# Staging places taken in the order of their last use, and the raw weights behind the change of MoE loaded at other times and from another queue

## The chip, the cores and the metric

The kernel runs on one core of a Trainium2 chip. The metric is the device time of one execution in microseconds (us), the median of several runs. The core has TensorE (PE in the profile), VectorE (DVE), ScalarE (ACT) and GpSimd (POOL), and SyncE (SP), which here only issues DMAs. A DMA can be issued by SP or by ACT. It then stands among that engine's own instructions: one that has to wait holds up all that stands behind it on the same engine.

## The reference

Attention over 4 batches of 576 tokens gives x (2304 x 512). A first mixture of experts (4 experts, width 1024, ReLU, outputs weighted by domain_probs) follows, and then one dense pair of layers of width 2048 with ELU, called the second MoE here.

```python
def _moe_ref(x, domain_probs, w1, w2) -> np.ndarray:
    ...
    for e in range(E):
        h = np.maximum(x @ w1[e], 0.0)
        out += p[:, e:e + 1] * (h @ w2[e])
    return out.astype(np.float32)
...
def _moe2_ref(x, w_in, w_out) -> np.ndarray:
    h = x @ w_in
    alpha = 1.0
    g = np.where(h > 0.0, h, alpha * (np.exp(np.minimum(h, 0.0)) - 1.0))
    return (g @ w_out).astype(np.float32)
```

## The kernel before

**Steps.** Attention and expert 0 come first. The rest is 30 steps, `i` = 0 to 29, in `STEPS`: step `i` is half unit `s` = i // 3 (512 hidden features: half an expert, or a quarter of the second MoE) for block `b` = i % 3 (768 tokens). `S_MOE` is 6, so steps 0 to 17 are experts 1 to 3 and steps 18 to 29 are the second MoE; the change of MoE is between steps 17 and 18. A step has two passes (`fp`) of seven Strassen products `p` = 0 to 6 (L996, 6 matmuls of 384 columns each) for the first layer. After products 1, 3 and 5 of each pass stands a `chunk` of the step before (L1043 to L1045, 12 matmuls of 512 columns: the second layer for 128 tokens).

**Hooks.** A chunk calls `hook2` four times, so a step has 24 hooks. `at2(i, k, fn)` puts `fn` at hook `k` of step `i`; `k` may run on into later steps, so that hook 42 set from step 18 is hook 18 of step 19. All work beside the products is spread over the engines in this way, and each engine runs its part in the order in which it was written.

**Precision.** Every fp32 operand is held as two parts, high and low: a copy to the rounded type (ACT or POOL) and a subtraction (DVE or POOL).

**The turn.** The second MoE needs the output of the first one transposed, in seven Strassen operands per block. `turn_steps(b, c)` makes them for nine groups of 128 + 128 tokens in steps 16 to 19: PE transposes (L837), ACT copies back (L838), POOL forms differences (L860), and `emit` splits an operand into high and low in a staging place (copy L845 or L847, subtraction L851) and stores it to `xs` in DRAM from SP (L852). There are 63 emits, numbered 0 to 62 here by `stage_n`. The subtraction and the store of one emit are written just ahead of the next hook function of the turn.

**Staging places.** `staged(n)` chooses the place of emit n. Up to the start of step 18 there are six places: `y`, `qh`, `ql`, the two halves of the tile `ek`, and a part of `extra`. From step 18 on, where ELU wants `y`, `qh`, `ql` and `extra` itself, there are four (the halves of `ek` and of one tile `r` of the pool `stg`), and from hook 9 of step 18 on six (a second `r`). The choice is `n % 6` or `n % len(stage)`. An emit waits until the last store from its place has landed.

**Ring loads.** `ring_load` (L664) brings a product's operand back from `xs`, high (`xh`) and low (`xl`) part, from SP. The seven of step i + 1 are issued in the second pass of step i: the first two at product 0, then one at each of products 1 to 5, so the one for product 5 at product 4. For the second MoE a ring load has to wait for the stores that it reads.

**Raw weights.** `w_load(s, p, layer)` (L679 to L683) loads a pair of raw weight tiles, 256 KB each, into an `r` of the same pool `stg`, which has two buffers; it is issued by ACT. `w1_steps` splits and combines the first layer's weights, `w2_step` the second layer's (copies on ACT, L735, subtractions on POOL, L736). In most half units the second layer's weights of s + 1 come first (loads at hooks 2 and 10, `w2_step` at 25 and 29) and the first layer's at 34 and 38. For s = 6 (`S_MOE`), both second-layer loads are at hook 42, right behind the last emit of the turn at hook 41, with `w2_step` at 47 and 49, and the first layer's loads at 52 and 54.

**ELU.** L1020 to L1031: three ACT functions of a PSUM bank, DVE combines, ACT and DVE split the result. The bank can be written by PE again when DVE has read it (L1026).

Of the kernel before, what the change touches and what calls it, by code (L numbers as in the profile page):

```python
# [9 lines left out]
F32R = mybir.dt.float32r  # L10
# [9 lines left out]
def tile_attention_moe_moe(  # L20
# [13 lines left out]
    nc = tc.nc  # L34
    NP_, CP, NC, P = q.shape
    D, S = P // 2, NC * CP
    NT, DM = out.shape
# [39 lines left out]
    TB, FS = 384, 4  # L77
    NB = NT // (2 * TB)
    STEPS = [(s, b) for s in range((NU - 1) * FPU // FS) for b in range(NB)]
    S_MOE = (E - 1) * FPU // FS  # L80
# [11 lines left out]
    stg = ctx.enter_context(tc.tile_pool(name="stg", bufs=2))  # L92
    hp_ = ctx.enter_context(tc.tile_pool(name="hp", bufs=1))
    kvp = ctx.enter_context(tc.tile_pool(name="kvp", bufs=1))
    tmp = ctx.enter_context(tc.tile_pool(name="tmp", bufs=1))
# [396 lines left out]
    def bank(which):  # L492
        pool = ps_h if which == "h" else ps[which]
        return pool.tile([P, ps["wide"] if which == "m" else 1, 512], F32, tag=which, name=which)
# [5 lines left out]
    t = bank("o")  # L500
# [62 lines left out]
    for i in range(NP_):  # L563
        late = i >= NPAIR
        t = K_START[i - NPAIR] if late else HALF_STEP * i
# [103 lines left out]
    def w_load(s, p, layer):  # L669

        if (s, p, layer) == (0, 1, 1):
            r = tmp.tile([P, 2, DM], F32, tag="ek", name="r")
        else:
            r = stg.tile([P, 2, DM], F32, tag="r", name="r")
        for j in range(2):
            u, c = divmod(FPU + s * FS + 2 * p + j, FPU)
            if u >= E:
                src = scratch[(u - E) * FPU + c, :, layer, :]
                nc.scalar.dma_start(out=r[:, j, :], in_=src)  # L679
            elif layer == 0:  # L680
                nc.scalar.dma_start(out=r[:, j, :].rearrange("p (d f) -> p d f", d=KD), in_=w1[u][c])
            else:
                nc.scalar.dma_start(out=r[:, j, :], in_=w2[u][c * P : (c + 1) * P, :])  # L683
        (w1r, w2r)[layer][s, p] = r

    def w1_steps(s, p):

        r, t = [], []

        def begin():  # L690
            r.append(w1r.pop((s, p)).rearrange("p j (d f) -> p j d f", d=KD))
            new()

        def new():
            t.extend(wp.tile([P, 2, KD, P], F32R, tag="w1", name="w1s") for _ in range(2))
            if len(t) == 4:
                w1s[s, p] = dict(
                    A11=(t[0], 0), A12=(t[0], 2), A22=(t[1], 0),
                    S2=(t[2], 0), S4=(t[2], 2), S3=(t[3], 0), S1=(t[3], 2),
                )  # L700

        def src(k):
            return (r[0][:, 0], r[0][:, 1, 2:], r[0][:, 0], r[0][:, 1])[k]

        def dst(k, hl):
            return t[k][:, hl, :2] if k == 1 else t[k][:, hl]

        def hi(k):
            nc.scalar.activation(out=dst(k, 0), in_=src(k), func=AF.Copy)

        tt = nc.vector.tensor_tensor

        def lo(k):
            tt(out=dst(k, 1), in0=src(k), in1=dst(k, 0).bitcast(F32), op=ALU.subtract)

        def sums1():
            f1, f2 = r[0][:, 0], r[0][:, 1]
            tt(out=f2[:, 2:], in0=f2[:, :2], in1=f2[:, 2:], op=ALU.add)
            tt(out=f2[:, :2], in0=f1[:, :2], in1=f2[:, :2], op=ALU.subtract)

        def sums2():
            f1, f2 = r[0][:, 0], r[0][:, 1]
            tt(out=f1[:, :2], in0=f2[:, 2:], in1=f1[:, :2], op=ALU.subtract)
            tt(out=f1[:, 2:], in0=f1[:, 2:], in1=f1[:, :2], op=ALU.subtract)

        return {
            0: lambda: (begin(), hi(1), hi(0)), 1: lambda: lo(1), 2: lambda: lo(0), 3: sums1, 4: lambda: (new(), hi(3)),
            5: lambda: (lo(3), sums2()), 6: lambda: hi(2), 7: lambda: lo(2),
        }

    def w2_step(s, p):
        r = w2r.pop((s, p))
        for j in range(2):
            t = wp.tile([P, 2, DM], F32R, tag="w2", name="w2s")
            nc.scalar.activation(out=t[:, 0], in_=r[:, j], func=AF.Copy)  # L735
            nc.gpsimd.tensor_tensor(out=t[:, 1], in0=r[:, j], in1=t[:, 0].bitcast(F32), op=ALU.subtract)  # L736
            w2s[s, 2 * p + j] = t


    SH = 24  # L740
# [3 lines left out]
    def at2(i, k, fn):  # L744
        timed2.setdefault(i * SH + k, []).append(fn)
# [6 lines left out]
    for b in range(NB):  # L752
        need = min(NP_, -(-2 * TB * (b + 1) // S) * NPAIR)
        t = 66 + 36 * b
# [22 lines left out]
    for i, (s, b) in enumerate(STEPS):  # L777
        more = s + 1 < len(STEPS) // NB
        if b == 0:
            for n, fn in w1_steps(s, 1).items():  # L780
                if s == 0 and n < 4:
                    at(204 + n, fn)
                else:
                    at2(i, n - 4 * (s == 0), fn)
        if not more:
            continue
        if b == 0:

            at2(i, 2 if s != S_MOE else 42, lambda s=s: w_load(s + 1, 0, 1))
            at2(i, 10 if s != S_MOE else 42, lambda s=s: w_load(s + 1, 1, 1))  # L790
            at2(i, SH + (1 if s != S_MOE else 23), lambda s=s: w2_step(s + 1, 0))
            at2(i, SH + (5 if s != S_MOE else 25), lambda s=s: w2_step(s + 1, 1))
            at2(i, SH + (10 if s != S_MOE else 28), lambda s=s: w_load(s + 1, 0, 0))
            at2(i, SH + (14 if s != S_MOE else 30), lambda s=s: w_load(s + 1, 1, 0))
        if b == 2:
            for n, fn in w1_steps(s + 1, 0).items():
                at2(i, 12 + n, fn)


    stage = []  # L800

    def staged(n):

        now = hook2_n[0] - NB * S_MOE * SH

        def two(pool, tag):
            t = pool.tile([P, 2, 2, 2 * P], F32R, tag=tag, name="stage")
            stage.extend([t[:, 0], t[:, 1]])

        if not stage:  # L810
            two(tmp, "ek")
        if now < 0:
            k = n % 6
            if k < 3:
                return tmp.tile([P, 2, 2 * P], F32R, tag=("y", "qh", "ql")[k], name="staged")
            if k == 5:
                return extra[:, TB : TB + DM].bitcast(F32R).rearrange("p (l n) -> p l n", l=2)
            return stage[k - 3]
        while len(stage) < (4 if now < 9 else 6):
            two(stg, "r")  # L820
        return stage[n % len(stage)]

    stage_n, stores = [0], []

# [4 lines left out]
    def turn_steps(b, c):  # L829
        j1, j2 = 6 * b + c, 6 * b + c + 3  # L830
        a1, a2 = acc(j1), acc(j2)
        q4 = {"B11": a1[:, : 2 * P], "B21": a1[:, 2 * P :], "B12": a2[:, : 2 * P], "B22": a2[:, 2 * P :]}

        def turn(a):
            t = bank("o")[:, 0, :]
            for d in range(KD):
                nc.tensor.transpose(t[:, d * P : (d + 1) * P], a[:, d * P : (d + 1) * P], ident)  # L837
            nc.scalar.activation(out=a, in_=t, func=AF.Copy)  # L838

        def emit(op, at_):  # L840
            t, x = staged(stage_n[0]), q4[at_]
            stage_n[0] += 1
            k, early = stage_n[0] % 7, hook2_n[0] < NB * S_MOE * SH
            if early or k % 2 == 0:
                nc.scalar.activation(out=t[:, 0], in_=x, func=AF.Copy)  # L845
            else:
                nc.gpsimd.tensor_copy(out=t[:, 0], in_=x)  # L847
            eng = nc.vector if early or k not in (1, 5) else nc.gpsimd

            def rest():  # L850
                eng.tensor_tensor(out=t[:, 1], in0=x, in1=t[:, 0].bitcast(F32), op=ALU.subtract)  # L851
                nc.sync.dma_start(  # L852
                    out=xs[1, b, OPS.index(op)].rearrange("p l (d n) -> p l d n", d=2)[..., c * P : (c + 1) * P],
                    in_=t.bitcast(F32).rearrange("p l (d n) -> p l d n", d=2),
                )

            stores.append(rest)

        def diff(o, x, y):
            nc.gpsimd.tensor_tensor(out=q4[o], in0=q4[x], in1=q4[y], op=ALU.subtract)  # L860

        return [
            lambda: turn(a1), lambda: turn(a2), lambda: emit("B11", "B11"), lambda: diff("B11", "B12", "B11"),
            lambda: emit("T1", "B11"), lambda: diff("B11", "B22", "B11"), lambda: emit("T2", "B11"),
            lambda: emit("B21", "B21"), lambda: (diff("B12", "B22", "B12"), diff("B21", "B21", "B11")),
            lambda: emit("T3", "B12"), lambda: emit("B22", "B22"), lambda: emit("T4", "B21"), lambda: None,
        ]

    for b in range(NB):
        i = NB * (S_MOE - 1) + b + 1  # L870
# [75 lines left out]
    for step in START.split():  # L946
        n, i = step[:-1], int(step[-1])
# [27 lines left out]
    extra = kvp.tile([P, NPAIR * 2 * P], F32, tag="kv", name="extra")  # L975
# [186 lines left out]
```

## Time and profile before

| | us |
|---|---|
| median of 3 runs (lowest to highest) | 1261.67 (1260.92 to 1263.71) |
| the profiled execution | 1260.91 |
| its span in the trace | 1259.1 |
| PE busy | 1217.0 |
| DVE / ACT / POOL busy | 804.4 / 505.5 / 190.0 |
| an undisturbed step (727.18 to 758.46) | 31.28 |

Times in the trace count from the span's start. "Busy" of PE includes time at a lower granted clock; the idle time of an engine matters only where PE waits for it. A step begins with the first matmul of its product 0; steps 15 to 21 begin at 727.18, 758.46, 791.51, 825.44, 869.67, 907.67 and 952.49.

### The profile page before, as it was taken

To read this page: it belongs to the slowest core of one execution; us is meant where nothing else is said; L and a number is where in the kernel's file an instruction comes from. 1 tells how busy PE (TensorE), PEld (TensorE's weight loads), DVE (VectorE), ACT (ScalarE), POOL (GpSimd) and SP (SyncE) were. 2 spreads that over 40 slices of the span, in tenths; PEclk is the share of its full clock that TensorE was granted. 3 is DMA by queue.
4 is the path that set the end of the run, shared out by engine and by line. 5 is a ranking of instruction groups with operands and counts; after the bars stand their busy time and mean duration, and the time that the engine had idled before them with its cause. 6 is when DMAs were issued, how large, how long until landed. Compare 5 with 4: busy or idle time off the path is not lost.

```text
span 1259.1 us, 18264 instructions
## 1 busy us (share of the span) xinstructions
PE 1217.0 (97%) x6526; PEld 1083.4 (86%) x6526; DVE 804.4 (64%) x1514; ACT 505.5 (40%) x1105; POOL 190.0 (15%) x194
## 2 busy tenths in 40 slices
PE   7799999999999999999999999989779999999998
PEld 6688889889999988999998999878678898998996
DVE  6866776356676676676676663666546567567564
ACT  6544553232222222222222222545466656556552
POOL 4522552011001001001001001244310100100000
PEclk8899999999999999999999999999989999999999
DMA  7434557628677677677677675879855556555541
GB/s 234 131 110 137 185 194 253 219 79 324 234 264 271 237 254 257 234 274 257 241 260 256 232 264 206 273 231 290 275 180 206 182 199 207 192 194 172 184 178 75
DMA packets 152603, 272.19 MB, mean 216 GB/s; under 512 B 12864, under 2 KB 72768, under 8 KB 152512
## 3 DMA queue, kind: packets, MB, share of 16 engines
q1 hardware_dynamic: 131776, 224.87, 52.0%
q10 hardware_dynamic: 20736, 46.15, 10.4%
q8 instruction: 52, 0.85, 0.3%
q14 instruction: 39, 0.32, 0.1%
HBM read 224.83 MB, written 46.14 MB: 215 GB/s over the span
## 4 chain that ended last, share of the span: by engine, by line
PE 86%; DVE 5%; DMA 3%; ACT 3%; issue 2%; SPq 1%; POOL 0%; ACTq 0%; POOLq 0%; DVEq 0%
PE m L996 16%; PE h L996 16%; PE o L1045 12%; PE o L1044 12%; PE o L1043 12%; PE o L879 7%; PE h L879 7%; DMA xs<-stage 2%; PE m L264 1%; PE m L356 1%; ACT t L1022 1%; PE m L333 1%; DVE g L1026 1%; PE o L837 0%; DMA r<-in_w_dram 0%
## 5 line engine op out<-in xcount | busy, mean ns | idle before, releaser
L996 PE MATMUL m<-xh,w1s 128*128 128x384 f32 x840 | 247.6, 341 | 17.2 <-DVE g L1026 10.5
L996 PE MATMUL h<-xh,w1s 128*128 128x384 f32 x840 | 246.0, 339 | 5.0 <-ACT m L1077 4.3
L996 PEld LDWEIGHTS m<-xh,w1s 128*128 128x128 f32 x840 | 156.3, 190 | 22.6 <-DVE g L1026 10.8
L996 PEld LDWEIGHTS h<-xh,w1s 128*128 128x128 f32 x840 | 155.4, 189 | 11.4 <-ACT m L1077 7.1
L736 POOL TENSOR_TENSOR w2s<-r,w2s 128x512 fp32r<-128x512 f32 x40 | 53.8, 1364 | 691.5 <-ACT w2s L735 480.9
L1043 PE MATMUL o<-w2s,xl 128*128 128x512 f32 x360 | 141.8, 394 | 1.8 <-ACT xl L1030 1.8
L1045 PE MATMUL o<-w2s,xl 128*128 128x512 f32 x360 | 142.9, 397 | 0.0
L996 PE MATMUL m<-xl,w1s 128*128 128x384 f32 x420 | 142.5, 339 | 0.0
L1044 PE MATMUL o<-w2s,xl 128*128 128x512 f32 x360 | 142.4, 395 | 0.0
L996 PE MATMUL h<-xl,w1s 128*128 128x384 f32 x420 | 141.5, 337 | 0.0
L1023 DVE SCALAR_TENSOR_TENSOR extra<-extra,t 128x384 f32<-128x384 f32 x96 | 54.2, 565 | 128.6 <-ACT t L1022 128.6
L879 PE MATMUL o<-w2t,hpa 128*128 128x512 f32 x432 | 118.0, 402 | 1.2 <-DVE hpa L911 1.0
L879 PE MATMUL h<-xh,w1t 128*128 128x256 f32 (+1 forms) x512 | 112.1, 298 | 0.1
L879 PEld LDWEIGHTS h<-xh,w1t 128*128 128x128 f32 x512 | 86.1, 192 | 5.2 <-POOL w1t L402 0.3
L879 PEld LDWEIGHTS o<-w2t,hpa 128*128 128x128 f32 x432 | 76.1, 190 | 15.1 <-DVE hpa L911 2.4
L996 PEld LDWEIGHTS m<-xl,w1s 128*128 128x128 f32 x420 | 79.8, 190 | 3.4
L996 PEld LDWEIGHTS h<-xl,w1s 128*128 128x128 f32 x420 | 79.3, 189 | 3.2
L1045 PEld LDWEIGHTS o<-w2s,xl 128*128 128x128 f32 x360 | 67.9, 189 | 16.2 <-DVE xl L1031 1.8
L1043 PEld LDWEIGHTS o<-w2s,xl 128*128 128x128 f32 x360 | 68.3, 190 | 15.5 <-ACT xl L1030 3.7
L1044 PEld LDWEIGHTS o<-w2s,xl 128*128 128x128 f32 x360 | 68.0, 189 | 12.1
L879 PE MATMUL h<-xl,w1t 128*128 128x256 f32 (+1 forms) x256 | 77.3, 302 | 0.0
L1051 DVE SCALAR_TENSOR_TENSOR accB<-o,pn,accB 128x512 f32<-128x512 f32 x60 | 44.9, 749 | 50.5 <-PE o L1045 50.4
(188 smaller groups left out, 2275.4 us busy)
## 6 DMA issues: line engine op xcount, KB each, us to landing
xh<-xs SPq DMA_DIRECT2D x210, 384.0 KB, 5.1
xl<-xs SPq DMA_DIRECT2D x210, 384.0 KB, 5.8
r<-in_w_dram ACTq DMA_DIRECT2D x48, 256.0 KB, 3.7
xs<-stage SPq DMA_DIRECT2D x47, 256.0 KB, 3.3
x<-in_w_in_dram ACTq DMA_DIRECT2D x16, 512.0 KB, 5.5
x<-in_w_out_dram ACTq DMA_DIRECT2D x16, 512.0 KB, 4.8
r<-scratch ACTq DMA_DIRECT2D x32, 256.0 KB, 3.7
xs<-xh SPq DMA_DIRECT2D x21, 384.0 KB, 3.6
```

Of the source, the lines that this page charges most:

```text
L264: nc.tensor.matmul(o, ek[:n, ks], vs, start=(c == 0), stop=(c == len(k_chunks) - 1))
L333: nc.tensor.transpose(t[:, a - halves[0], c * CP : (c + 1) * CP], qt[:CP, 3 * a + c, :], ident[:CP, :CP])
L356: nc.tensor.matmul(t[:, a, :HALF], kv[:, l, :], r[:, a, :], start=(n == 0), stop=(n == 2))
L736: nc.gpsimd.tensor_tensor(out=t[:, 1], in0=r[:, j], in1=t[:, 0].bitcast(F32), op=ALU.subtract)
L879: nc.tensor.matmul(out, lhsT, rhs, **kw)
L996: nc.tensor.matmul(dst, t[:, wl, c + dl, :], x[xl_][:, dl, :], start=(n == 0 and p < 2), stop=(n == 5), skip_group_check=True,)
L1022: nc.scalar.activation(out=t, in_=m, func=AF.Tanh, scale=-0.5)
L1023: nc.vector.scalar_tensor_tensor(out=e_, in0=e_, scalar=1.0, in1=t, op0=ALU.add, op1=ALU.mult)
L1043: nc.tensor.matmul(o, gh, w[:, 0, :], start=(f == 0), stop=False)
L1044: nc.tensor.matmul(o, gh, w[:, 1, :], start=False, stop=False)
L1045: nc.tensor.matmul(o, gl, w[:, 0, :], start=False, stop=(f == FS - 1))
L1051: nc.vector.scalar_tensor_tensor(out=a, in0=o, scalar=pn[:, j, e : e + 1], in1=a, op0=ALU.mult, op1=ALU.add)
```

## The change

Three things are changed.

1. `staged` no longer counts. It keeps the places in a list, takes the first and puts it at the end, so that the place used longest ago is next. In the first phase the order becomes `y`, `qh`, `ql`, `extra`, `ek`, `ek`. When the tile `r` comes in, its halves go to the front of the list.
2. For the half unit behind the change of MoE (s + 1 = 7), the loads of the first layer's raw weights come first, both at hook 42; the second layer's come later, at hooks 70 and 82, with their `w2_step` at 77 and 91. For s + 1 = 8 the second layer's loads move from hooks 2 and 10 to 21 and 23, the `w2_step` from 25 and 29 to 29 and 33, and the first layer's loads from 34 and 38 to 38 and 42.
3. The loads of the first layer's raw weights for half unit 7 are issued by SP and not by ACT.

```diff
+        q = nc.sync if (s, layer) == (S_MOE + 1, 0) else nc.scalar
         for j in range(2):
...
-                nc.scalar.dma_start(out=r[:, j, :], in_=src)
+                q.dma_start(out=r[:, j, :], in_=src)
...
-            at2(i, 2 if s != S_MOE else 42, lambda s=s: w_load(s + 1, 0, 1))
...
+            a2, b2, c2, d2, a1, b1 = (2, 10, 25, 29, 34, 38)
+            if s == S_MOE:
+                a1, b1, a2, c2, b2, d2 = (42, 42, 70, 77, 82, 91)
+            elif s == S_MOE + 1:
+                a2, b2, c2, d2, a1, b1 = (21, 23, 29, 33, 38, 42)
+            at2(i, a2, lambda s=s: w_load(s + 1, 0, 1))
...
-        if now < 0:
-            k = n % 6
-            if k < 3:
-                return tmp.tile([P, 2, 2 * P], F32R, tag=("y", "qh", "ql")[k], name="staged")
-            if k == 5:
-                return extra[:, TB : TB + DM].bitcast(F32R).rearrange("p (l n) -> p l n", l=2)
-            return stage[k - 3]
-        while len(stage) < (4 if now < 9 else 6):
-            two(stg, "r")
-        return stage[n % len(stage)]
...
+        if "ek" in stage:
+            stage[-1:] = two(tmp, "ek")
+        if now >= 0 and any(isinstance(t, str) for t in stage):
+            stage[:] = two(stg, "r") + [t for t in stage if not isinstance(t, str)]
+        if now >= 9 and len(stage) == 4:
+            stage[:0] = two(stg, "r")
+        t = stage.pop(0)
+        stage.append(t)
```

The first place is on ACT at the start of step 18, where the number of places changes: `stage_7033` is the tile `ek`, `stage_7472` the first `r`; the three stage rows are emits 24, 26 and 27 (emit 25 is copied by POOL). Before:

```order
L709 ACTIVATE w1s_7461<-r_6982 128x512
L845 ACTIVATE stage_7033<-accA_92 128x256
L838 ACTIVATE accB_93<-o_7477 128x512
L845 ACTIVATE stage_7472<-accA_92 128x256
L838 ACTIVATE accB_93<-o_7493 128x512
L845 ACTIVATE stage_7472<-accB_93 128x256
L1020 ACTIVATE m_7519<-h_2832 128x384
```

With the change the same rows of ACT read:

```order
L710 ACTIVATE w1s_7461<-r_6982 128x512
L851 ACTIVATE stage_7472<-accA_92 128x256
L844 ACTIVATE accB_93<-o_7477 128x512
L851 ACTIVATE stage_7033<-accA_92 128x256
L844 ACTIVATE accB_93<-o_7493 128x512
L851 ACTIVATE stage_7033<-accB_93 128x256
L1026 ACTIVATE m_7519<-h_2832 128x384
```

Emits 24 and 25 now have the new tile, and emits 26 and 27 the two halves of `ek`, which emits 22 and 23 (before: 21 and 22) used last. The order of the work itself is the same. From emit 34 on both kernels go through six places in the same order.

The second place is ACT behind the last emit (62), at hook 18 of step 19. Before (`r_8118` and `r_8121` are the raw weights of half unit 7, `w2s` their split second layer):

```order
L845 ACTIVATE stage_7472<-accB_93 128x256
L679 DMA r_8118<-scratch 128x512 x2
L679 DMA r_8121<-scratch 128x512 x2
L1055 ACTIVATE accA_92<-o_8103 128x512
L1020 ACTIVATE m_8143<-m_2834 128x384
L1021 ACTIVATE extra_2836<-m_8143 128x384
L1022 ACTIVATE t_8144<-m_8143 128x384
L1030 ACTIVATE hpa_94<-g_8099 128x384
L735 ACTIVATE w2s_8168<-r_8118 128x512
```

With the change ACT goes from the copy of emit 62 to the evacuation of a chunk (L1061, before L1055) at once, and the loads stand on SP, between the last two stores of the turn (L858) and the ring loads of products 5 and 6 of step 20:

```order
L858 DMA xs<-stage_7033 512x1x128
L858 DMA xs<-stage_7472 512x1x128
L680 DMA r_8118<-scratch 128x512 x2
L680 DMA r_8121<-scratch 128x512 x2
L664 DMA xh_90<-xs 128x768
L664 DMA xl_91<-xs 128x768
L664 DMA xh_90<-xs 128x768
L664 DMA xl_91<-xs 128x768
```

The four loads have left ACT, and the ring loads that follow have four DMAs more ahead of them on SP. The loads of `r_8121` take the buffer of `stage_7472`, the place of emit 62.

The third place is ACT in the second pass of step 21 with the change, where the second layer's weights of half unit 7 are split (`w2s`, from `r_8604`) and those of half unit 8 are loaded (`r_8752`, `r_8761`); before, nothing but rows of the ELU and L1055 stood here:

```order
L736 ACTIVATE w2s_8711<-r_8604 128x512
L736 ACTIVATE w2s_8714<-r_8604 128x512
L1061 ACTIVATE accB_93<-o_8698 128x512
L1026 ACTIVATE m_8733<-m_2834 128x384
L1027 ACTIVATE extra_2836<-m_8733 128x384
L1028 ACTIVATE t_8734<-m_8733 128x384
L1036 ACTIVATE hpa_94<-g_8694 128x384
L680 DMA r_8752<-scratch 128x512 x2
L680 DMA r_8761<-scratch 128x512 x2
```

ACT issues the two pairs of loads close together there; the second pair takes the buffer that POOL frees when it has split `r_8604`.

## Rows read from the trace of the kernel before

**Rows 1.** The profile's page: the span, and the chain that ended last by engine.

```profile
span 1259.1 us, 18264 instructions
...
PE 86%; DVE 5%; DMA 3%; ACT 3%; issue 2%; SPq 1%; POOL 0%; ACTq 0%; POOLq 0%; DVEq 0%
```

**Rows 2.** Windows, steps 15, 17, 18, 19, 20, 21: length, busy, clock, DMA.

```profile
core 0: us, PE busy (x) PEld busy (x) DVE busy (x) ACT busy (x) POOL busy (x), PEclk, DMA share, GB/s
727.18:758.46 31.28, 31.28 (x157) 28.22 (x157) 19.29 (x37) 7.64 (x16) 0.00 (x0) 1.00 0.70 253
...
791.51:825.44 33.93, 33.93 (x181) 30.55 (x181) 23.08 (x48) 17.80 (x44) 9.15 (x12) 1.00 0.89 283
825.44:869.67 44.23, 37.87 (x181) 33.24 (x181) 29.67 (x53) 23.04 (x54) 19.82 (x27) 0.92 0.81 251
869.67:907.67 38.00, 34.11 (x165) 30.25 (x165) 21.43 (x39) 19.66 (x47) 15.40 (x22) 0.96 0.88 270
907.67:952.49 44.82, 34.36 (x158) 30.20 (x158) 19.71 (x39) 26.10 (x57) 5.04 (x4) 0.85 0.66 219
952.49:985.04 32.55, 32.01 (x157) 27.98 (x157) 19.11 (x37) 21.02 (x47) 0.00 (x0) 1.00 0.59 199
```

**Rows 3.** Timeline of PE: start, us, instruction, idle before it and its releaser.

```profile
839.30 0.45 PE L996 MATMUL m<-xh,w1s 128*128 128x384 f32 x1 [3.09 <-DVE h L1079]
...
847.23 0.44 PE L996 MATMUL m<-xh,w1s 128*128 128x384 f32 x1 [1.26 <-DVE m L1083]
...
919.34 0.69 PE L996 MATMUL m<-xh,w1s 128*128 128x384 f32 x1 [10.46 <-DVE g L1026]
```

**Rows 4.** Timeline of ACT around the loads of half unit 7.

```profile
901.02 0.40 ACT L845 ACTIVATE stage<-accB 128x256 fp32r<-128x256 f32 x1
905.22 10.42 ACTq L679 DMA_DIRECT2D r<-scratch  x4
915.69 0.60 ACT L1055 ACTIVATE accA<-o 128x512 f32<-128x512 f32 x1 [14.27 <-DMA xs<-stage]
...
917.96 1.13 ACT L735 ACTIVATE w2s<-r 128x512 fp32r<-128x512 f32 x2
```

**Rows 5.** Windows: the stretch behind PE's longest wait, columns as in group 2.

```profile
919.40:924.80 5.40, 5.40 (x14) 4.67 (x15) 2.72 (x6) 4.36 (x12) 1.75 (x2) 0.50 0.73 281
```

**Rows 6.** Timeline of SP: stores and the ring load behind them, steps 18 and 19.

```profile
865.86 1.21 SPq L852 DMA_DIRECT2D xs<-stage  x2
870.37 0.33 SPq L664 DMA_DIRECT2D xh<-xs  x1
...
905.88 0.32 SPq L664 DMA_DIRECT2D xh<-xs  x1
...
906.78 1.22 SPq L852 DMA_DIRECT2D xs<-stage  x2
914.07 0.33 SPq L664 DMA_DIRECT2D xh<-xs  x1
```

**Rows 7.** The chain that ended last: the turn's last store, issue and time to landing.

```profile
907.36 7.41 DMA xs<-stage
```

**Rows 8.** DMA issues of 914.0 to 914.8: KB, us from issue to landing.

```profile
xl<-xs SPq DMA_DIRECT2D x1, 384.0 KB, 3.6
```

**Rows 9.** Timeline of ACT at the start of step 18 (emits 24, 26 and 27).

```profile
834.36 0.42 ACT L845 ACTIVATE stage<-accA 128x256 fp32r<-128x256 f32 x1 [5.33 <-DMA xs<-stage]
...
835.16 0.41 ACT L845 ACTIVATE stage<-accA 128x256 fp32r<-128x256 f32 x1
...
835.95 0.41 ACT L845 ACTIVATE stage<-accB 128x256 fp32r<-128x256 f32 x1
```

**Rows 10.** Timeline of POOL there (emit 25).

```profile
835.19 0.90 POOL L847 CAST stage<-accA 128x256 fp32r<-128x256 f32 x1 [7.22 <-DMA xs<-stage]
```

**Rows 11.** Timeline of DVE there.

```profile
835.76 0.62 DVE L851 TENSOR_TENSOR stage<-accA,stage 128x256 fp32r<-128x256 f32 x1
...
838.69 0.55 DVE L1079 TENSOR_TENSOR h<-m,extra 128x384 f32<-128x384 f32 x1
...
845.62 0.42 DVE L851 TENSOR_TENSOR stage<-accB,stage 128x256 fp32r<-128x256 f32 x1 [1.08 <-ACT stage L845]
```

**Rows 12.** The page's costliest groups: busy us, mean ns, idle before.

```profile
L736 POOL TENSOR_TENSOR w2s<-r,w2s 128x512 fp32r<-128x512 f32 x40 | 53.8, 1364 | 691.5 <-ACT w2s L735 480.9
```

More of the change, by code (lines that the diff above doesn't have):

```diff
@@ L787, in tile_attention_moe_moe @@
         if b == 0:
-            at2(i, 2 if s != S_MOE else 42, lambda s=s: w_load(s + 1, 0, 1))
[L790 to L794, printed above, removed]
+            a2, b2, c2, d2, a1, b1 = (2, 10, 25, 29, 34, 38)
[4 more added lines that the diff above has]
+            at2(i, a2, lambda s=s: w_load(s + 1, 0, 1))
+            at2(i, b2, lambda s=s: w_load(s + 1, 1, 1))
+            at2(i, c2, lambda s=s: w2_step(s + 1, 0))
+            at2(i, d2, lambda s=s: w2_step(s + 1, 1))
+            at2(i, a1, lambda s=s: w_load(s + 1, 0, 0))
+            at2(i, b1, lambda s=s: w_load(s + 1, 1, 0))
         if b == 2:
@@ L797, in tile_attention_moe_moe, with staged @@
                 at2(i, 12 + n, fn)
-    stage = []
-    def staged(n):
+    stage = ["y", "qh", "ql", "extra", "ek"]
+    def staged():
         now = hook2_n[0] - NB * S_MOE * SH
@@ L807, in two @@
             t = pool.tile([P, 2, 2, 2 * P], F32R, tag=tag, name="stage")
-            stage.extend([t[:, 0], t[:, 1]])
-        if not stage:
-            two(tmp, "ek")
-        if now < 0:
-            k = n % 6
-            if k < 3:
-                return tmp.tile([P, 2, 2 * P], F32R, tag=("y", "qh", "ql")[k], name="staged")
-            if k == 5:
-                return extra[:, TB : TB + DM].bitcast(F32R).rearrange("p (l n) -> p l n", l=2)
-            return stage[k - 3]
-        while len(stage) < (4 if now < 9 else 6):
-            two(stg, "r")
-        return stage[n % len(stage)]
+            return [t[:, 0], t[:, 1]]
+        if "ek" in stage:
[6 more added lines that the diff above has]
+        stage.append(t)
+        if t == "extra":
+            return extra[:, TB : TB + DM].bitcast(F32R).rearrange("p (l n) -> p l n", l=2)
+        return tmp.tile([P, 2, 2 * P], F32R, tag=t, name="staged") if isinstance(t, str) else t
     stage_n, stores = [0], []
@@ L840, in emit @@
         def emit(op, at_):
-            t, x = staged(stage_n[0]), q4[at_]
+            t, x = staged(), q4[at_]
             stage_n[0] += 1
```

## The prediction

> **What bounds the kernel now.** I began with the page. The chain that ended last lies on PE for 86% of the span [rows 1], so what can be won is the time in which PE waits or runs slowly, and the question is where that is. The windows by step answer it [rows 2]. A bare step takes 31.28 us at full clock, and step 17, with 24 transposes more and no wait, takes 33.93. Step 18 takes 44.23, step 19 takes 38.00, step 20 takes 44.82, step 21 takes 32.55. So the change of MoE costs 10.3 us over step 17 in step 18, some 6 in step 19, 13.54 over a bare step in step 20 and 1.27 in step 21, with the granted clock at 0.92, 0.96 and 0.85 in the first three. All three parts of the change lie in this stretch.
>
> Then I asked the timeline of PE what ended its waits [rows 3]. The longest is in step 20: 10.46 us, ended by DVE at L1026, which reads the bank that PE wants to write. DVE is only the messenger. The timeline of ACT shows the cause [rows 4]: after the copy of emit 62 at 901.02 it does nothing for 14.27 us, until 915.69; in between stand its four loads of raw weights, and the releaser is the landing of a store from a staging place. ACT is in order, so the evacuation (L1055) and the ELU behind it wait for a buffer that they don't need, and PE waits for the ELU. After the wait PE runs 5.40 us at a granted clock of 0.50, the 1.2 GHz level [rows 5], and does in that time what it does in 2.7 at full clock: 10.46 + 2.7 = 13.2 of the 13.54.
>
> **The change, part by part.**
>
> *The loads leave ACT.* This takes the 14.27 us from ACT, and with them the 13.54 from step 20, if nothing takes their place. The transfers themselves were never needed early (the weights are split at hook 47 at the earliest). What is behind them now is SP. There the second pair of loads waits for the landing of the last store of the turn, since it takes its buffer, and behind it stand the ring loads of products 5 and 6 of step 20. Is product 5 late? The last store leaves at 907.36 [rows 7]. Its landing took 7.41 us, with two loads of ACT beside it, which now come after it. Two stores behind a ring load in step 18 with no such loads were read 4.5 us after the first had left (865.86 to 870.37), against 7.3 in step 19 (906.78 to 914.07) [rows 6]. I take 4.5: landed at 911.9. Two issues of SP take 1.2 (906.78 has two in 1.22), the high part of the ring load 0.6 more, so its low part leaves at 913.7. Landing takes from 3.6 us, when little is in its way [rows 8], to 7.4, as for the last store; with two loads of 256 KB ahead I take 4.6, so 918.3. When does PE want it? A step has 14 products of 6 x 384 columns and 6 chunks of 12 x 512, 69,120 columns in 31.28 us. Ahead of product 5 of the first pass stand five products and two chunks, 23,808 columns, 10.8 us: from 907.67 that is 918.4. So it is just in time; I enter 0.3 us for the wait. The bounds are no wait, and with both landings at 7.4 us 914.8 + 1.8 + 7.4 = 924.0, a wait of 5.6. With 0.2 for small change, step 20 gives back 13.0.
>
> *The order of the places.* What changes is the turn-over at the start of step 18. Before, emit 24 on ACT waited 5.33 us for the store of emit 21, until 834.36 [rows 9], and emit 25 on POOL 7.22 for that of emit 22, until 835.19 [rows 10]. With the change both have a new tile and need not wait. But emits 26 and 27, two rows further on the same ACT, now have the places of emits 22 and 23, whose stores are the same ones at the same time: landed at about 835.15 and, one store later, 0.8 on, at about 836.0. Before, ACT copied emit 26 at 835.16 and emit 27 at 835.95 [rows 9]. So ACT reaches the ELU behind them at the same time, and the stall has only moved two rows down. DVE stands in order too: its subtraction of emit 26 came at 835.76 [rows 11] and can't come before 835.6, and L1079 at 838.69, which ended PE's 3.09 us [rows 3], follows it by the same rows. I count 0.2 there. Further on, DVE waited 1.08 us at 845.62 for ACT's copy of emit 31 [rows 11], which in both kernels waits for the store of emit 27; that store can be up to 1 us earlier, because POOL has emit 25 behind it by then and disturbs DVE less, and the 1.26 us that PE waited at 847.23 [rows 3] may shrink by as much. I enter 0.9 for both. The bounds are nothing and the whole 10.3 of step 18. From emit 34 on the order of places is the same, so step 19 keeps its 38.00, give or take 1.
>
> *The loads and splits at other hooks.* The second layer's weights of half unit 7 are now split in step 21: four copies on ACT, 1.13 a pair [rows 4], and four subtractions on POOL of 1.36 [rows 12]. ACT is busy 21.02 of 32.55 there and POOL not at all [rows 2]. The load at hook 82 wants the buffer that the split at 77 frees, the one at 95 that of the split at 91. A hook is 31.28 / 24 = 1.3 us, so they have 6.5 and 5.2 us for 1.1 + 2.7 = 3.8: covered, by 1.4 at the closer. Where that cover is gone, ACT stands again, and ELU behind it. The weights of the last split are wanted by the chunks of step 22, five hooks and two products later, some 8 us. I enter 0.4 us for the fuller step 21 (its 1.27 over a bare step are what the first layer's splits cost there, so nothing to 2).
>
> **The sum** is made against the profiled execution: 1260.91 - 13.0 - 0.9 + 0.4 = 1247.4. The median of the runs is 0.76 above that execution, so 1248.2.
>
> **A rule that speaks against it.** The Trainium skill, "DMA: Bandwidth & Descriptors", section "Issuing engines are not separate DMA queues", says that all DMAs run on the same 16 engines whoever starts them, and that starting them on several engines "will only save the time on the sequencer it takes to initiate the DMA". By that the move of the loads would be worth four issues; its time is the third rival. The trace does not agree so far, since ACT stood 14.27 us ahead of these issues and not in them.
>
> **The rivals.**
> 1. *SP becomes the place of the wait.* The store lands late, the ring loads come behind 1 MB of weights, and PE waits at product 5. For it: stores and loads took about 7 us in this stretch [rows 6, 7]. Against: the loads that made it so are now behind the store. Its time goes from a wait of 1.8 us (store at 7.4, ring load at 3.6) to 5.6 with 2.7 for the clock: 1250 to 1256, middle 1252.5. Chance 0.17.
> 2. *The new order frees step 18.* If the stores of emits 22 and 23 land earlier than I think, the three waits and the slow clock go, and step 18 falls to 33.93: 9.4 more, 1239. Against: ACT's next rows wait for the same stores. Chance 0.08.
> 3. *Only the issue is saved.* ACT is freed, but PE waits as long for something that now waits on SP. Four issues of 0.6 are 2.4 us: 1261.67 - 2.4 = 1259.3. Chance 0.04.
> 4. *Slower: ACT waits in step 20 to 22.* The four new pairs of loads at hooks 70, 82, 93 and 95 stand on ACT behind DVE, POOL and landings. A microsecond of ACT's wait cost 13.54 / 14.27 = 0.95 in step 20. It decides from 13.5 / 0.95 = 14.2 us over all four, 3.6 at each. At 4.5 each, a store's landing, it is 17 us: 1265. Against: the covers above. Chance 0.03.
>
> **The numbers.** The forecast, 1248.2, has 0.65 and by itself 1245.5 to 1250.5; the rest, 0.03, is for nothing won or lost at all. The range is 1243 to 1254: it takes in the forecast, most of the first rival and half of the way to the second. No change is within 0.2%, 2.5 us, about what a measurement can tell here. Faster: the forecast and rivals 1 and 2, 0.90; the same, rival 3 and the remainder, 0.06 (a little of each goes to slower); slower 0.04.
>
> **What would show it.** Right: ACT has no idle time of over 2 us between its copy of emit 62 and the next evacuation; PE's 10.46 us are gone and step 20 takes 31.3 to 32.5 at a clock of 1.00; steps 18 and 19 still take 42.5 to 44 and 37 to 38.5, and ACT's wait for a store at about 829 to 835 is still there, one stage row later. Wrong: step 20 with a wait of PE at product 5 of the first pass, released by a DMA (rival 1); step 18 under 38 (rival 2); ACT idle behind L680 in steps 20 to 22 (rival 4).

## The result, and the profile after

| | before | after |
|---|---|---|
| median of 4 runs each on one chip (lowest to highest), us | 1261.89 (1260.92 to 1263.71) | 1251.03 (1248.84 to 1252.83) |
| ratio (95% interval) | | 0.9915 (0.990 to 0.993) |
| the profiled execution / its span | 1260.91 / 1259.1 | 1251.63 / 1249.9 |

The kernel is 10.9 us faster. Its time is 2.8 us above the forecast of 1248.2 and inside the range. The windows of the steps answer to [rows 2]; here are steps 18 to 22 after the change (the columns are those of that group):

```profile
827.24:872.23 44.99, 37.82 (x182) 33.28 (x181) 30.29 (x53) 22.70 (x54) 19.35 (x27) 0.92 0.82 251
872.23:908.24 36.01, 32.75 (x165) 28.76 (x165) 23.04 (x42) 22.96 (x54) 15.34 (x22) 1.00 0.90 281
908.24:940.14 31.90, 31.90 (x157) 27.96 (x157) 18.37 (x36) 21.07 (x47) 0.00 (x0) 1.00 0.82 275
940.14:974.62 34.48, 32.47 (x157) 27.84 (x157) 21.07 (x37) 22.23 (x50) 5.54 (x4) 1.00 0.54 190
974.62:1007.34 32.72, 32.01 (x158) 27.97 (x158) 19.08 (x34) 18.99 (x43) 5.10 (x4) 1.00 0.63 226
```

Step 20 has gone from 44.82 us at a clock of 0.85 to 31.90 at 1.00, with PE busy in all of it: 12.9 us. Step 18 is 0.8 longer, step 19 2.0 shorter; steps 21 and 22 (32.55 and 31.63 before) are 1.9 and 1.1 longer. The sum is 11.1 us, and the other steps are as they were.

The timelines of ACT and of SP at the end of the turn, which answer to [rows 4] and [rows 6], show how:

```profile
901.59 0.40 ACT L851 ACTIVATE stage<-accB 128x256 fp32r<-128x256 f32 x1
902.51 0.60 ACT L1061 ACTIVATE accA<-o 128x512 f32<-128x512 f32 x1 [0.52 <-PE o L1051]
```

```profile
906.85 1.21 SPq L858 DMA_DIRECT2D xs<-stage  x2
908.11 4.65 SPq L680 DMA_DIRECT2D r<-scratch  x4
912.87 0.36 SPq L664 DMA_DIRECT2D xh<-xs  x1
913.27 0.43 SPq L664 DMA_DIRECT2D xl<-xs  x1
```

Between the copy of emit 62 and the evacuation ACT is now idle for 0.52 us, waiting for PE, where it stood 14.27. The wait for the store's landing is still there, but in SP's four loads, which take 4.65 us to issue, 2.1 of them waiting (what SP waited for, 903 to 916); the ring load of product 5 leaves behind them. Its two parts landed 5.5 and 6.1 us after their issue:

```profile
xh<-xs SPq DMA_DIRECT2D x1, 384.0 KB, 5.5
xl<-xs SPq DMA_DIRECT2D x1, 384.0 KB, 6.1
```

So they were there at 918.4 and 919.4. By the prediction's count of columns PE wants them at 908.24 + 10.8 = 919.0. In the trace it begins product 5 at 919.39 and first reads the low part here:

```profile
919.57 0.34 PE L1002 MATMUL h<-xl,w1s 128*128 128x384 f32 x1
```

That is just in time, by 0.2 us, and PE did not wait in step 20.

The turn-over at the start of step 18, which answers to [rows 9] and [rows 3], first on ACT and then on PE:

```profile
837.56 0.42 ACT L851 ACTIVATE stage<-accA 128x256 fp32r<-128x256 f32 x1 [5.61 <-DMA xs<-stage]
...
846.99 0.42 ACT L851 ACTIVATE stage<-accB 128x256 fp32r<-128x256 f32 x1 [2.16 <-DMA xs<-stage]
```

```profile
840.83 0.45 PE L1002 MATMUL m<-xh,w1s 128*128 128x384 f32 x1 [2.82 <-DVE h L1085]
849.05 0.45 PE L1002 MATMUL m<-xh,w1s 128*128 128x384 f32 x1 [1.54 <-DVE m L1089]
858.03 0.44 PE L1002 MATMUL h<-xh,w1s 128*128 128x384 f32 x1 [2.81 <-ACT m L1083]
```

ACT's wait of 5.33 us at emit 24 has become one of 5.61 at emit 26, two rows down, and PE's first two waits are of the size that they had (3.09 and 1.26). The third was 2.02 and is 2.81, the 0.8 us by which step 18 is longer.

The extra time of step 21 is in the timelines of DVE, POOL and ACT around hook 77:

```profile
950.92 1.80 DVE L715 TENSOR_TENSOR w1s<-r,w1s 128x512 fp32r<-128x512 f32 x1
952.65 1.52 DVE L724 TENSOR_TENSOR r<-r 128x256 f32<-128x256 f32 x1
```

```profile
950.88 3.00 POOL L737 TENSOR_TENSOR w2s<-r,w2s 128x512 fp32r<-128x512 f32 x2 [55.31 <-ACT w2s L736]
```

```profile
954.66 0.63 ACT L710 ACTIVATE w1s<-r 128x512 fp32r<-128x512 f32 x1 [3.33 <-DVE r L725]
```

POOL's two subtractions run beside two rows of DVE that belong to the first layer's weights. In the kernel before the same two rows, in the same step, took 0.68 and 0.42:

```profile
963.58 0.68 DVE L714 TENSOR_TENSOR w1s<-r,w1s 128x512 fp32r<-128x512 f32 x1
964.18 0.42 DVE L723 TENSOR_TENSOR r<-r 128x256 f32<-128x256 f32 x1
```

So DVE is 2.2 us late, ACT waits 3.33 us for it ahead of a copy, and the ELU stands behind that copy.

### The profile page after: what moved, and what is told of

The parts are those of the page before. It is cut to its first block, busy times and chain, and to the rows that moved or that the text cites. A ratio compares the mean times of both kernels' runs of the same rounds, so it can differ in the third digit from the quotient of the medians.

```text
span 1249.9 us, 18268 instructions
## 1 busy us (share of the span) xinstructions
PE 1216.1 (97%) x6526; PEld 1081.5 (87%) x6526; DVE 809.6 (65%) x1514; ACT 505.6 (40%) x1105; POOL 189.6 (15%) x194
## 4 chain that ended last, share of the span: by engine, by line
PE 85%; DVE 5%; DMA 3%; ACT 3%; issue 2%; ACTq 0%; SPq 0%; POOL 0%; DVEq 0%; POOLq 0%
PE m L1002 16%; PE h L1002 16%; PE o L1051 12%; PE o L1050 12%; PE o L1049 12%; PE o L885 7%; PE h L885 7%; DMA xs<-stage 1%; DMA accB<-in_v_dram 1%; PE m L356 1%; ACT t L1028 1%; PE m L264 1%; DVE g L1032 1%; DMA x<-in_w_in_dram 1%; PE m L333 1%
```

## The experiments

My theory was that ACT, in order, stood behind a landing, that taking the loads from it was nearly all of the gain, and that the order of places gained nothing much. The rivals: the order of places or of layers does it, or only the issue is saved. Each run compares with the kernel before on the same chip. The columns "from 16" give the span less the start of step 16, ahead of which no kernel here differs from another; steps 18 to 22 are lengths from the trace, in us. The kernel before had a median of 1262.19 beside the first four experiments, 1262.09 beside the next three and 1260.97 beside the last two.

| kernel | median | ratio (95% interval) | from 16 | 18 | 19 | 20 | 21 | 22 |
|---|---|---|---|---|---|---|---|---|
| before | 1261.89 | | 1259.1 - 758.46 = 500.6 | 44.23 | 38.00 | 44.82 | 32.55 | 31.63 |
| after | 1251.03 | 0.9915 (0.990 to 0.993) | 1249.9 - 760.26 = 489.6 | 44.99 | 36.01 | 31.90 | 34.48 | 32.72 |
| e1_places | 1260.32 | 0.9983 (0.997 to 0.9996) | 1258.5 - 759.53 = 499.0 | 43.56 | 38.98 | 42.83 | 32.21 | 31.66 |
| e2_loads | 1252.6 | 0.9925 (0.9902 to 0.9948) | 1249.7 - 758.89 = 490.8 | 42.27 | 39.64 | 31.86 | 34.49 | 32.89 |
| e3_act | 1262.51 | 0.9999 (0.9985 to 1.0014) | 1258.4 - 758.76 = 499.6 | 43.67 | 35.68 | 43.42 | 34.44 | 32.64 |
| e4_sp_only | 1258.03 | 0.9973 (0.9958 to 0.9988) | 1256.0 - 759.24 = 496.8 | 43.12 | 39.37 | 40.87 | 32.27 | 31.63 |
| e5_ring | 1249.11 | 0.9895 (0.9879 to 0.9912) | 1245.9 - 758.84 = 487.1 | 39.86 | 38.43 | 31.88 | 34.45 | 32.84 |
| e6_hooks | 1251.22 | 0.9908 (0.9893 to 0.9922) | 1248.2 - 760.62 = 487.6 | 42.53 | 38.08 | 32.46 | 32.94 | 32.09 |
| e7_ring2 | 1247.94 | 0.9883 (0.9868 to 0.9898) | 1245.5 - 758.39 = 487.1 | 39.95 | 38.61 | 31.86 | 34.50 | 32.55 |
| e8_both | 1247.76 | 0.9895 (0.9879 to 0.9912) | 1246.2 - 760.08 = 486.1 | 40.11 | 38.70 | 32.68 | 32.96 | 32.10 |
| e9_old_places | 1245.12 | 0.9874 (0.9859 to 0.9888) | 1243.4 - 759.03 = 484.4 | 39.16 | 38.74 | 31.90 | 32.95 | 32.12 |

Two things in this table bound what may be read from it. Step 16 starts at 758.39 to 760.62, 2.2 us apart, in kernels that do the same up to there. And `after` and `e3_act` do the same work in the same order up to late in step 19, yet their steps 18 and 19 take 81.0 and 79.4 together. Differences of 2 us in one trace are not worth a story.

**The order of places alone.** On the kernel before:

```diff
-            t, x = staged(stage_n[0]), q4[at_]
+            t, x = staged(), q4[at_]
```

with the new `staged` and nothing else of the change.

> The kernel before with the new order of places alone; the loads stay on ACT at hook 42. Theory (the order only moves ACT's wait two stage rows down): 1260 to 1263 us, nothing that can be told from the kernel before; ACT waits some 5.5 us for a store ahead of emit 26 in place of emit 24, step 18 stays at 44 to 45 us, step 20 at 44 to 45 with PE's wait of 10 us in it. Rival (the order frees something): 1255 or less, with step 18 or step 19 at least 2 us shorter than before.

1260.32 us, 2 below the kernel before, with an interval that ends just under 1. ACT's wait is at emit 26, as the theory says:

```profile
837.64 0.42 ACT L844 ACTIVATE stage<-accA 128x256 fp32r<-128x256 f32 x1 [6.42 <-DMA xs<-stage]
```

Step 18 is 0.7 shorter and step 19 1.0 longer; the 2.0 us that it is ahead are in step 20, where PE's long wait is still there with 8.84. Both steps are shorter than the 44 to 45 that I gave, and ACT's wait is longer than the 5.5. Nothing is freed in step 18, so the rival falls. What the 2 us are was not settled.

**The loads alone.** On the changed kernel:

```diff
-            t, x = staged(), q4[at_]
+            t, x = staged(stage_n[0]), q4[at_]
```

with the old `staged`.

> The changed kernel with the old order of places: the loads of half unit 7 in the new order, at the new hooks and from SP. Theory: all of the gain is here, 1250 to 1252 us, with step 20 at 31.3 to 32.5 us and steps 21 and 22 some 3 us longer in sum than before; ACT's wait is back at emit 24. Rival (the order of places carries part of it): 1254 or more.

1252.6 us: 0.9925 where the whole change has 0.9915. From step 16 on it has 9.8 of the 11.0 us, and the order of places alone has 1.6; the two add up to the whole. Step 20 is at 31.86, and steps 21 and 22 carry the same 3 us as after. The median is 0.6 above the range that I gave; the intervals of the two overlap, so a small share of the order of places stays possible.

**The loads back on ACT.** On the changed kernel:

```diff
-        q = nc.sync if (s, layer) == (S_MOE + 1, 0) else nc.scalar
+        q = nc.scalar
```

> The changed kernel with one thing undone: the loads of the first layer for half unit 7 are issued by ACT again, at the same hook 42. Theory (ACT, in order, stands behind the landing of the last stores): ACT stands 10 to 14 us between the copy of emit 62 and the next evacuation, PE waits 8 to 11 us in step 20 with a stretch at half clock behind it, and the time is 1261 to 1266, as long as before or up to 4 longer, since steps 21 and 22 keep their 3 us. Rival (the other order of the two layers and the new hooks free step 20, the queue doesn't matter): 1250 to 1253. Rival (only four issues of some 0.6 are saved by SP): 1253.5.

1262.51 us, ratio 0.9999: the whole gain is gone. ACT's timeline, and then PE's, in step 20:

```profile
902.68 9.73 ACTq L680 DMA_DIRECT2D r<-scratch  x4
912.46 0.60 ACT L1061 ACTIVATE accA<-o 128x512 f32<-128x512 f32 x1 [13.63 <-DMA xs<-stage]
```

```profile
916.11 0.69 PE L1002 MATMUL m<-xh,w1s 128*128 128x384 f32 x1 [9.82 <-DVE g L1032]
```

ACT stands 13.63 us, PE 9.82, and step 20 takes 43.42. One word in the program, the queue of four DMAs, is worth 0.0084 x 1262 = 10.6 us. The order of layers and the hooks don't free step 20 by themselves, and it is not four issues of 0.6 either. The Trainium skill, "DMA: Bandwidth & Descriptors", section "Issuing engines are not separate DMA queues", prices another issuing engine at the sequencer's time to start the DMA; this run does not agree for an issue that has to wait, since all that stands behind it on the engine waits too.

**The queue alone.** On the kernel before, for the second layer's loads at hook 42:

```diff
+        q = nc.sync if (s, layer) == (S_MOE + 1, 1) else nc.scalar
...
-                nc.scalar.dma_start(out=r[:, j, :], in_=src)
+                q.dma_start(out=r[:, j, :], in_=src)
```

> The kernel before with the queue alone changed: the second layer's loads at hook 42 are issued by SP, but their splits stay at hooks 47 and 49. Theory (the queue alone doesn't do it, since ACT's copies of these weights now wait for their landing): the loads leave SP at some 907.5 and 912 and land at 913 and 917, and ACT stands there for them with the ELU behind it, 10 us or more in all; step 20 stays over 40 us and the time is 1255 to 1262. Rival (leaving ACT is all that counts): 1248 to 1250, below the changed kernel, since steps 21 and 22 stay as before.

1258.03 us: 4 of the 11. ACT is not held by the issue any more, but by the copies that read these weights at hook 47 (ACT, then PE):

```profile
914.21 1.27 ACT L736 ACTIVATE w2s<-r 128x512 fp32r<-128x512 f32 x2 [7.19 <-DMA r<-scratch]
```

```profile
917.78 0.80 PE L1044 MATMUL o<-w2s,xl 128*128 128x512 f32 x1 [5.44 <-ACT xl L1031]
```

I had counted 10 us of waiting for the two pairs; the first cost 7.19 and the second none, being landed by then. So both halves are needed: the queue, and another order in which nobody wants the data soon.

**Step 18: the stores ahead of the ring loads**

Neither order of places frees step 18, since the stores land late. Why do they? SP's timeline after the change, what SP waited for from 825 to 831, and a row of DVE:

```profile
828.22 0.33 SPq L664 DMA_DIRECT2D xh<-xs  x1
828.59 0.43 SPq L664 DMA_DIRECT2D xl<-xs  x1
829.12 0.37 SPq L664 DMA_DIRECT2D xh<-xs  x1
829.54 0.42 SPq L664 DMA_DIRECT2D xl<-xs  x1
830.06 0.53 SPq L858 DMA_DIRECT2D xs<-extra  x1
830.68 0.59 SPq L858 DMA_DIRECT2D xs<-stage  x1
```

```profile
SPq L664 <- DMA xs<-staged: 3.1, 1, 3.1
```

```profile
825.50 0.43 DVE L857 TENSOR_TENSOR stage<-accA,stage 128x256 fp32r<-128x256 f32 x1 [2.87 <-ACT stage L851]
```

The last row is DVE's subtraction of emit 22: it is ready at 825.93, and its store leaves at 830.68. In between SP stands, until 828.2, ahead of the ring load of product 5, which waits 3.1 us for the landing of an earlier store; then it issues this ring load, that of product 6 and the store of emit 21. It is the same fault as on ACT, one queue further. So in the changed kernel these two ring loads are moved behind the three stores:

```diff
-                        ring_load(len(OPS) * (i + 1) + p + 1)
+                        n = len(OPS) * (i + 1) + p + 1
+                        if i in (17,) and p >= 4:
+                            at2(i + 1, 0, lambda n=n: ring_load(n))
+                        else:
+                            ring_load(n)
```

> The changed kernel with one thing more: at the end of step 17 the ring loads of products 5 and 6 of step 18, which wait on SP for the stores of emits 19 and 20, are issued at hook 0 of step 18, so that the stores of emits 21, 22 and 23, which stood behind them on SP, go first. Theory (what ACT waits for in step 18 is not the transfer of a store but its late issue behind those ring loads: emit 22 was ready at 825.9 and its store left at 830.7): these stores leave at some 825, 826 and 829 and land by 829 to 833, ACT's wait of 5.61 us at emit 26 falls under 1 us, PE's waits in step 18 (7.2 us) and its half clock fall by half or more, step 18 takes 36 to 41 us and the time is 1243 to 1248. Rival (the wait goes on to the next places, emits 28 to 31, or PE now waits for the ring loads at product 5): step 18 over 43, 1249 to 1253.

Step 18 falls from 44.99 to 39.86. The stores of emits 22 and 23 leave at 824.53 and by 828.1 (SP), and ACT copies emits 26 and 27 at 830.42 and 831.56 without waiting:

```profile
824.53 3.50 SPq L858 DMA_DIRECT2D xs<-stage  x2
828.13 0.57 SPq L664 DMA_DIRECT2D xh<-xs  x1
```

```profile
830.42 0.41 ACT L851 ACTIVATE stage<-accA 128x256 fp32r<-128x256 f32 x1
...
831.56 0.41 ACT L851 ACTIVATE stage<-accB 128x256 fp32r<-128x256 f32 x1
```

ACT's wait is gone, as I held, and the rival falls for step 18. But I had put it all down to the late issue, and the store of emit 22 is also quicker here: it left 4.7 us earlier, counted from the start of step 18 (1.3 us ahead of it, at 824.53, and not 3.4 behind it, at 830.68), and it landed 4.9 us after its issue and not 6.8, as it did behind the ring loads in the changed kernel (the DMA views, first of the changed kernel, then of this run):

```profile
xs<-stage SPq DMA_DIRECT2D x1, 256.0 KB, 6.8
```

```profile
xs<-stage SPq DMA_DIRECT2D x1, 256.0 KB, 4.9
```

PE's waits in step 18 fall from 7.2 to 4.0 us, a little less than by half. The time, 1249.11, is above the range that I gave, because step 19 took 38.43 here, at a clock of 0.96.

**The same for step 19.** On the kernel of the run before:

```diff
-                        if i in (17,) and p >= 4:
+                        if i in (17, 18) and p >= 4:
```

> As the run before with the ring loads of step 18 issued at its hook 0, and the same for step 19 (its ring loads of products 5 and 6 at hook 0 of step 19, with five stores ahead of them in place of two). Theory: step 19 too loses part of its 3.3 us of waits, since the store of emit 42 was ready at 866.1 and left at 876.2: 33 to 35 us, and the time is 0 to 3 us below that of the run with step 18 alone. Rival (the ring loads of step 19 now stand behind the store of emit 44, which was ready at 877.3, and come late): step 19 takes 37 us or more, 1 to 4 us above that run.

Step 19 takes 38.61. The theory falls (33 to 35); of the rival the length is there, but no loss against the run before (38.43). The stores of emits 40 to 42 leave in time now. But the ring loads leave at 871.02 to 873.03 (SP), and a store right behind them, which left at 873.71, took 6.7 us to land. ACT waits 5.00 us for it:

```profile
880.52 0.42 ACT L851 ACTIVATE stage<-accB 128x256 fp32r<-128x256 f32 x1 [5.00 <-DMA xs<-stage]
```

From step 16 on the two runs are equal, 487.1, and the intervals of their ratios overlap. Nothing can be told for or against this edit.

**Steps 21 and 22: other hooks.** On the changed kernel:

```diff
-                a1, b1, a2, c2, b2, d2 = (42, 42, 70, 77, 82, 91)
+                a1, b1, a2, c2, b2, d2 = (42, 42, 70, 82, 82, 91)
...
-                a2, b2, c2, d2, a1, b1 = (21, 23, 29, 33, 38, 42)
+                a2, b2, c2, d2, a1, b1 = (25, 28, 34, 38, 41, 45)
```

> The changed kernel with other hooks for the second layer: for half unit 7 the first w2_step at hook 82 in place of 77, so that POOL's subtractions no longer run beside DVE's sums of the first layer; for half unit 8 the loads at 25 and 28, the w2_step at 34 and 38 and the first layer's loads at 41 and 45. Theory (step 21 lost 1.9 us because POOL's two subtractions at 950.9 to 953.9 made DVE's rows L715 and L724 take 1.80 and 1.52 in place of some 0.7 and 0.4, and step 22 lost 1.1 because ACT stood 1.44 us behind loads that were issued too close together): steps 21 and 22 fall from 34.5 and 32.7 to 32 to 33 and 31.3 to 32, and the time is 1.5 to 3 us below the changed kernel. Rival (these 3 us are the price of the copies on ACT): no difference.

Steps 21 and 22 take 32.94 and 32.09 in place of 34.48 and 32.72: 2.2 of the 3.0 us come back, a little less than expected in step 22. DVE's two rows are as short as before the change:

```profile
951.46 0.68 DVE L715 TENSOR_TENSOR w1s<-r,w1s 128x512 fp32r<-128x512 f32 x1
952.05 0.42 DVE L724 TENSOR_TENSOR r<-r 128x256 f32<-128x256 f32 x1
```

So the disturbance by POOL is shown. The copies on ACT are still in these steps, so they can be no more than the 0.8 us that are left. Just ahead of step 22 ACT no longer stands behind the loads: the row that waited 1.44 us now waits 0.82, for PE. The median, 1251.22 and 0.9908, doesn't show these 2 us apart from the change's 0.9915; from step 16 on they are there (487.6 to 489.6).

**Both, and both with the old order of places.** `e8_both` is `e7_ring2` with the hooks of `e6_hooks`; `e9_old_places` differs from it by the old `staged` alone:

```diff
-            t, x = staged(), q4[at_]
+            t, x = staged(stage_n[0]), q4[at_]
```

> The changed kernel with both: the ring loads of products 5 and 6 at hook 0 of steps 18 and 19, and the other hooks for the second layer of half units 7 and 8. Theory (the two act in different steps and add up): step 18 at 40, steps 21 and 22 at 33 and 32, the time 1245 to 1247, some 1.5 to 2 us below the run with the ring loads alone and some 5 below the changed kernel. Rival (what is won in step 21 comes back as a wait elsewhere): 1248 or more.

> The run with both and the old order of places. Theory (the order of places decides only which emit waits for a store, and the stores of emits 21 to 23, which leave early here, are landed for either): the same time within 1.5 us. Rival (the new order gives each place one more emit of time, which the kernel before could not use because the stores left late): 2 us or more longer, with step 18 over 41 us and ACT waiting for a store at emits 24 to 27.

`e8_both` took 1247.76 us, just over the range given. Its ratio is no better than that of `e7_ring2` (0.9895 and 0.9883, with intervals that overlap), and from step 16 on it is 1.0 us shorter in place of 1.5 to 2, so that the two add up is not shown in the time. The steps are as expected (40.11, 32.96, 32.10), but step 20 took 32.68, with a wait of PE of 0.41 us for the ring load of product 5:

```profile
917.85 0.44 PE L1002 MATMUL h<-xl,w1s 128*128 128x384 f32 x1 [0.41 <-DMA xl<-xs]
```

`e9_old_places` took 1245.12 us, ratio 0.9874, the fastest kernel here, 16 us below the kernel before and some 5 below the change. It is 2.6 below `e8_both`, more than the 1.5 that I allowed, and on the other side of the rival. All four of its runs (1244.63 to 1245.45) lie below all four of `e8_both` (1247.22 to 1248.84), so this is more than scatter between runs. But of the 2.8 us between the two spans 1.05 lie ahead of step 16, where both do the same, 0.95 in step 18 and 0.78 in step 20. Two kernels can thus differ by 1 us where their work is the same, and that the order of places makes the rest is not shown. That the new order is not needed, once the stores leave early, is.

## Why the prediction was right, and where it was off

**The loads leave ACT: right, in mechanism and in size.** I forecast 13.0 us in step 20; it is 12.9. The store landed as I had entered it (two stores with a median of 4.4 us). The ring load of product 5 took 5.5 and 6.1 us to land and not 4.6, but its low part left 5.0 us into the step (913.27 - 908.24) and not 6.0 (913.7 - 907.67), and PE's wait was 0 and not 0.3. That a landing 1.5 us slower and an issue 1.0 us earlier nearly cancel is luck. How near it was is shown by `e6_hooks` and `e8_both`, where PE did wait for it, 0.29 and 0.41 us: rival 1 has the right place, and its price there is far under the 1.8 to 5.6 us that I gave it.

**The stall of step 18 moves two rows down: right.** 5.61 us at emit 26, in `after` and (6.42) in `e1_places`. **The 0.9 us that I gave this term rest on a step that failed:** I held that the store of emit 27 would be up to 1 us earlier, so that the wait at emit 31 would shrink. The first half came: the store left at 841.21 before and at 842.22 after, which is 15.8 and 15.0 us into step 18, and DVE's subtraction ahead of it was no longer slowed. The second did not. The store took 4.7 us to land in place of 3.9, so it landed 19.7 us into the step in both kernels, and ACT, which came earlier, waited 2.16 us in place of 1.35. Before (rows of DVE, SP and ACT):

```profile
840.30 0.84 DVE L851 TENSOR_TENSOR stage<-accB,stage 128x256 fp32r<-128x256 f32 x1
```

```profile
841.21 0.51 SPq L852 DMA_DIRECT2D xs<-stage  x1
```

```profile
845.17 0.42 ACT L845 ACTIVATE stage<-accB 128x256 fp32r<-128x256 f32 x1 [1.35 <-DMA xs<-stage]
```

After (DVE's row, where the subtraction takes 0.42 us, and the chain of waits):

```profile
841.74 0.42 DVE L857 TENSOR_TENSOR stage<-accB,stage 128x256 fp32r<-128x256 f32 x1
```

```profile
842.22 4.68 DMA xs<-stage
```

I had taken the landing to be as long as before; why it was longer was not tried.

Step 18 got 0.8 longer and step 19 2.0 shorter; their sum, 1.2, is near the 0.9, but by no merit of mine, since that is within what two traces of the same work differ by.

**The loads and splits at other hooks: the term was too small.** I entered 0.4 us for step 21, nothing to 2, and no term for step 22; it measured 1.9 + 1.1 = 3.0 us, above the upper bound. I had counted the work (copies on ACT, subtractions on POOL), found POOL idle, and checked that buffers come free in time. I had not asked what POOL's rows do to DVE beside them, though the term of the places uses just this: the `w2_step` at hook 77 falls on the last hooks of the `w1_steps` of the first layer. `e6_hooks`, which moves it five hooks, gave back 1.5 us in step 21. Also, the load at hook 82 follows the first layer's splits, not that of hook 77 as I wrote: it left at 956.25, when DVE had ended the last row of those at 956.01. That cost nothing.

**The sum.** -12.9 - 1.2 + 3.0 = -11.1 us against -13.5 forecast; the difference of 2.4 is the third term, which is 2.6 larger than I entered.

**The signs.** Of what I named as signs of being right, the idle time of ACT, step 20 and the wait one stage row later came. The lengths of steps 18 and 19 did not: I gave 42.5 to 44 and 37 to 38.5, and they are 44.99 and 36.01.

**The rivals.** Rival 2 fell: step 18 was not freed by the order of places, and `e5_ring` shows what it needed, the stores earlier on SP. Rival 3 fell with `e3_act`. Rival 4 happened at a small size: ACT stood 3.33 us in step 21, behind DVE and not behind its own loads, and 1.44 us behind the loads at hooks 93 and 95 (ACT's timeline), in sum far under the 14 us from which it decides.

```profile
974.37 0.60 ACT L1061 ACTIVATE accB<-o 128x512 f32<-128x512 f32 x1 [1.44 <-DMA xh<-xs]
```

The releaser named there is the landing of a ring load, whose data has nothing to do with these loads. Why they wait for it was not tried.

## What to carry to other kernels

A DMA that has to wait costs what stands behind it on its engine, so look for long idle times that end at a landing, and ask who else stands there: here it was ACT's ELU for 13 us, and one queue further SP's stores for 5. Moving the issue helps only if the data is wanted late as well: the queue alone gave 4 of 11 us, the order alone none. And when work is moved to an idle engine, check which rows of a busy one then run beside it.

## What the runs showed of the hardware that was not expected

POOL's subtraction of 128x512 slows DVE beside it, and is slowed itself: DVE's rows L715 and L724 took 1.80 and 1.52 us beside it and 0.68 and 0.42 without, and POOL's pair 3.00 us beside them and 2.54 apart from them in `e6_hooks`. There POOL's pair runs beside an ELU row of DVE, one of whose inputs is a bank of PSUM, and that row keeps its usual 0.56 us (timelines of POOL and DVE, `e6_hooks`):

```profile
956.45 2.54 POOL L737 TENSOR_TENSOR w2s<-r,w2s 128x512 fp32r<-128x512 f32 x2 [60.92 <-ACT w2s L736]
```

```profile
956.53 0.56 DVE L1032 SCALAR_TENSOR_TENSOR g<-h,extra 128x384 f32<-128x384 f32 x1
```

The Trainium skill, "GPSIMD Engine Reference", section "1. Specifications", states that GpSimd's interfaces to SBUF are shared with VectorE, with contention for VectorE's instructions that have two inputs in SBUF. The traces agree: the two slowed rows read `r` and `w1s`, or `r` twice, from SBUF. Had I weighed that rule, the third term would have been larger.

The granted clock did not fall in step 19 of every trace. With a wait of PE of 2.84 us in its second pass and one of 0.42 nine us earlier, `after` kept full clock; with 2.83 and one of 1.25 nine us earlier, `e5_ring` ran at 0.50, the 1.2 GHz level, for the next 3.4 us, which costs some 1.7. The windows behind the longer wait, first of `after`, then of `e5_ring`:

```profile
897.40:901.00 3.60, 3.60 (x19) 3.33 (x20) 1.62 (x4) 2.19 (x6) 0.00 (x0) 1.00 1.01 400
```

```profile
892.40:895.70 3.30, 3.30 (x12) 3.20 (x11) 0.92 (x3) 0.58 (x2) 0.00 (x0) 0.50 1.01 398
```

Step 19 takes 35.7 and 36.0 us in the two traces that kept the clock, and 38.0 to 39.6 in the nine that did not. The clock is some 1.7 of the 2.0 to 4.0 us between them, and longer waits of PE are the rest. Which way it goes was not controlled by any edit here, and it is as large as what several of them were worth.
